# Phase tiles in a pool of their own, reused at the end for the last chunk's transform constants

## The chip, the cores and the metric

The kernel runs on one core of a Trainium2 chip. The metric is device time in microseconds (us), as the median of several executions; lower is better. One execution was also recorded by the hardware profiler, and that recording is what "the profile" and "the trace" mean below.

## What is computed

The reference is one transformer-like block on a sequence of 2048 rows of 640 features, in float32:

```python
mod = (_silu(c) @ w_mod).reshape(c.shape[0], 6, 1, -1)
sa, ca, ga, sb, cb, gb = (mod[:, 0], mod[:, 1], mod[:, 2], mod[:, 3], mod[:, 4], mod[:, 5])
h = _layernorm(x, axis=-1) * (1 + ca) + sa
x = x + ga * _A_ref(h, A_A_re, A_A_im, A_B_re, A_B_im, A_C_re, A_C_im, A_log_dt, A_Dskip)
h = _layernorm(x, axis=-1) * (1 + cb) + sb
x = x + gb * _B_ref(h, B_w1, B_w3, B_w2)
```

`_A_ref` builds for each of the 640 features a convolution kernel K of length 2048, a sum over 128 complex exponentials, and convolves the sequence with it by Fourier transforms. `_B_ref` is a gated feed-forward layer with 1728 hidden units (`silu(h w1) * (h w3)`, then `w2`).

## The kernel before

**Stages.** The time falls into a front (parameters, first normalization), the convolution, and the feed-forward part. The convolution writes its result `zs` to device memory; the feed-forward part starts with reading it back.

**The convolution's two streams.** One stream makes the kernel K, 16 features a step, in 40 steps (`NS`), after the front in rounds of 4 steps whose order of instructions is written out by hand (the string `ROUND`). For two steps at a time GpSimd makes integer phases (`phases`, tile `ph`, 32 x 67 values per partition), ScalarE turns them into sines in place and into cosines (`cs`), and VectorE multiplies them into the exponentials `A` (the words A1 and A2, `imag1` and `imag2`; A2 of the odd step is the last reader of a phase tile). TensorE sums these (`kg`, tile `pk`), and two more steps bring the kernel's transform into `uk`. There are 20 phase tiles in 3 buffers, in the pool `tp`, which the tables share.

The other stream is the transform itself, for 5 chunks of 128 features, 8 ticks a chunk, one tick a step, 10 steps behind (`LAG`): tick g of chunk c runs at step 10 + 8c + g. A tick is

- `stage2`: 16 matmuls of `uk` with the constant `s2` of that g, into `p2`;
- `k_copy` on ScalarE (tile `kc`), `products` and `sums` on VectorE (`T`, `p2`, `Y`);
- `inverse1`: 16 matmuls of `Y` with the constant `i1` of that g, into `pz`;
- `z_store`: ScalarE copies `pz` into `zt` (2 buffers), and a DMA stores it to `zs`.

Chunks 0 to 3 and tick 0 of chunk 4 run inside the rounds, beside the kernel's steps. Ticks 1 to 7 of chunk 4, the last chunk, run after the rounds, in a loop of their own, with nothing beside them but the first pieces of the feed-forward part (`x_part`).

**The constants.** `s2` and `i1` depend on g alone, 256 KB each. Each is loaded anew for every tick by `stage2_load` and `inverse1_load`, from SyncE's queue (`nc.sync`), into a pool of 2 buffers (`fp`). A load therefore has to wait until the tick two before it has used its constant. The dictionary `ahead` lets a load be made earlier: `stage2` and `inverse1` first look there.

**Names in the profile.** Digits are dropped from names there, so `s2` reads `s`, `i1` reads `i`, `p2` reads `p`. Most instructions carry line 109 (a helper); loads of `s2` carry L686, of `i1` L692, the loads `uk<-us` of the next chunk's input L678, the stores `zs<-zt` L766 (and, for the last chunk, ScalarE's queue).

**Orders.** Computing engines keep the program's order in this stretch. SyncE's DMAs are placed in its queue by the scheduler, and SyncE issues them strictly one after another: where one waits, those behind it wait too. After the last `i1` come, tied to it by `issue_after`, the first two weight tiles (`rw`) and two tiles of `x` (`xm`).

**Memory.** Pools are stacked from both ends: `tp` on the left, gone when the steps are done (`tabs.close()`); `kp`, then `fp`, on the right, gone when the convolution is done (`ssm.close()`). The feed-forward pools `xp` and `wq` are laid over them.

Of the kernel before, what the change touches and what calls it, by code (L numbers as in the profile page):

```python
# [9 lines left out]
F32 = mybir.dt.float32  # L10
F32R = mybir.dt.float32r
I32 = mybir.dt.int32
# [5 lines left out]
P = 128  # L18
# [5 lines left out]
NDC = D // DC  # L24
SD = 16
# [9 lines left out]
NPG = NPH + NG - 1  # L35
# [56 lines left out]
def bc(ap, axis, n):  # L92
    v = ap.unsqueeze(axis)
    shape = list(v.shape)
    shape[axis] = n
    return v.broadcast_to(shape)
# [18 lines left out]
def tile_kernel(ctx: ExitStack, tc: tile.TileContext, a):  # L115
    nc = tc.nc
# [22 lines left out]
    def keep(ins):  # L139

        return tc.keep_in_program_order(ins) if in_order[0] else ins
# [22 lines left out]
    ssm = ExitStack()  # L164
# [7 lines left out]
    one4 = kp.tile([P, 1], F32, name="one4")  # L172
    cT = kp.tile([P, KD], F32, name="cT")
    uk = kp.tile([P, 3, NA, DC], F32, name="uk")

    psS = ssm.enter_context(tc.tile_pool(name="psS", bufs=1, space=PSUM))

# [2 lines left out]
    tp = tabs.enter_context(tc.tile_pool(name="tp", bufs=2, reuse_waits="tile"))  # L180
# [251 lines left out]
    def late_load(i):  # L432

        late[i] = w_load(xw[:, :KD * WC].rearrange("p (k c) -> p k c", k=KD), 1920 + i * WC)
# [108 lines left out]
    ph, cs, AA, EC, PK, K1 = {}, {}, {}, {}, {}, {}  # L543
# [39 lines left out]

    def phases(s):
        sl = slice(s * SD, s * SD + 2 * SD)
        p = tp.tile([P, 2 * SD, NPG], I32, name="ph", bufs=3)
        hold = tc.keep_in_program_order if 0 < s < 4 else keep
        b0 = NA - 8
        base = p[:, :, b0:NA]
        hold(G.tensor_tensor(p[:, :, b0:], bc(thi[:, sl], 2, NPG - b0), bc(iota, 1, 2 * SD), op=OP.mult))  # L590
        keep(G.tensor_tensor(base, base, bc(phi[:, sl], 2, 8), op=OP.add))
        keep(G.tensor_tensor(p[:, :, :b0].rearrange("p k (g j) -> p k g j", j=8), bc(base, 2, NG - 1),
                             bc(p[:, :, NPH:], 3, 8), op=OP.add))
        ph[s] = p[:, :, :NPH]
# [86 lines left out]
    ahead = {}  # L681
# [7 lines left out]
    def inverse1_load(g):  # L689

        i1 = fp.tile([P, 2, 2, P], F32, name="i1")
        i1_last[0] = nc.sync.dma_start(i1, a["i1"][:, g * 2:g * 2 + 2])  # L692
        return i1

    def stage2(ch, g):
        s2 = ahead.pop((ch, g, "s2"), None)
        if s2 is None:
            s2 = stage2_load(g)
        kn = 1 + ch % 2

        n = ch * 8 + g
        p2 = psS.tile([P, 2, 2, 2 * DC], F32, name="p2", tag="B" if n > NS - 12 and n % 2 else "A", bufs=1)
        for pi in range(2):
            for c in range(2):
                for par in range(2):
                    f = g * 4 + pi * 2 + par
                    keep(PE.matmul(p2[par * 64:par * 64 + 64, pi, c, :], s2[:, pi * 2 + par, c * 64:c * 64 + 64],
                                   uk[:, 0:kn + 1:kn, f, :], start=True, stop=True, tile_position=(0, par * 64)))
        Pq[ch, g] = p2
        if g % 2 == 1 and ch + 1 < NDC:  # L710
            u_load(ch + 1, g // 2)
# [26 lines left out]
    def inverse1(ch, g):  # L738
        i1 = ahead.pop((ch, g, "i1"), None)
        if i1 is None:  # L740
            i1 = inverse1_load(g)
        Y = Yq.pop((ch, g))
        if g % 2 == 0:
            Zq[ch] = psS.tile([P, 2, 4, DC], F32, name="pz", tag="Z", bufs=1)
        pz = Zq[ch]
        for pi in range(2):
            for c in range(2):
                for par in range(2):
                    r = slice(par * 64, par * 64 + 64)
                    ins = keep(PE.matmul(pz[:, par, (g % 2) * 2 + pi, :], i1[r, pi, c, :], Y[r, pi, c, :],  # L750
                                         start=(c == 0), stop=(c == 1), tile_position=(par * 64, 0)))
        return ins
# [34 lines left out]
    def z_load(z, j, ks, q=nc.sync, b0=0):  # L787

        nb = z.shape[1]
        for k in ks:  # L790
            hh = int(k > 1)
            kk = k - 2 * hh
            q.dma_start(z[hh * 64:hh * 64 + 64, :, kk * DC:kk * DC + DC],
                        zsv[:, 4 * j + b0:4 * j + b0 + nb, k])
# [7 lines left out]
    def z_tile():  # L802
        z = tz.tile([P, SD, 3, NA], F32, name="A")
        return z.rearrange("p k s b -> p (k s b)").rearrange("p (b d) -> p b d", b=4)
# [15 lines left out]
    def x_load(j):  # L820
        xe.append(xw[:, j * D:(j + 1) * D])
        nc.sync.dma_start(xe[j], a["x"][j * P:(j + 1) * P, :])
# [21 lines left out]
    def conv_part(fn):  # L844
        return lambda k: fn((k - LAG) // 8, (k - LAG) % 8)

    parts = {"PH": phases, "AB": absph, "CO": cosine, "SI": sine, "PA": lambda k: exp_fast((k,)), "XA": fast,
             "PQ": lambda k: exp_slow((k,)), "XQ": slow, "E1": real1, "E2": real2, "A1": imag1, "A2": imag2,
             "kg": kgen, "K": k1evac, "pt": k_stage1, "uk": k_out}
# [5 lines left out]
    def do(name, k):  # L855

        lo, hi = (LAG, LAG + 8 * NDC) if name in conv else (0, NS)
        if name in by_two and k % 2:
            return None
        if front[0]:  # L860
            assert (name, k) not in done and lo <= k < hi, (name, k)
        if (name, k) in done or not lo <= k < hi or (name == "zt" and k % 2 == 0 and k < LAG + 8 * NDC - 8):
            return None
        done.add((name, k))
        return (conv if name in conv else parts)[name](k)
# [20 lines left out]
    def u_first(i):  # L886

        u_load(0, i)
        if i == 0:
            ahead[0, 1, "s2"] = stage2_load(1)  # L890
            for g in range(2):
                ahead[0, g, "i1"] = inverse1_load(g)
# [45 lines left out]
    for word in FRONT:  # L938
        name, k = word[:2].rstrip("+"), int(word[len(word[:2].rstrip("+")):])
# [25 lines left out]
    for rnd in range(NS // EB):  # L965
        if 2 <= rnd < 7:
            late_load(rnd - 2)
        for word in ROUND:
            name, k = word[:2].rstrip("+-"), EB * rnd + int(word[len(word[:2].rstrip("+-")):])
            if name in pieces:  # L970
                if 2 <= rnd < 7:
                    pieces[name](rnd - 2)
                continue
            do(name, k)
            if name == "E1" and 30 <= k < 38 and k % 2 == 0:
                x_load((k - 30) // 2)

            if name == "kg" and 36 <= k < 40:
                early.append((None, z_tile()))
                z_load(early[-1][1], k - 36, range(3), q=nc.gpsimd)  # L980
    in_order[0] = False

    for tk in range(NS + 1, LAG + 8 * NDC + 2):
# [13 lines left out]
        i = tk - 1 - LAG - 8 * NDC + 8  # L997
# [190 lines left out]
    ahead = {(0, n): w for n, w in first_w.items()}  # L1188
# [272 lines left out]
    for pair in range(2):  # L1461
# [4 lines left out]
        side = []  # L1466
# [8 lines left out]
        if pair == 0:  # L1475
            tiles = []
            power = x_first(tiles)
            for k in range(KD):
# [12 lines left out]
            side = [lambda: mid(0), lambda: (mid(1), mid(2)), lambda: mid(3), lambda: None,  # L1491
                    lambda: turn(4, 0, 2), lambda: turn(3, 1)]
# [106 lines left out]
```

## Time and profile before

| | us |
|---|---|
| runs: median (lowest to highest of 3) | 943.66 (943.36 to 947.34) |
| profiled execution, first to last instruction | 944.4 |
| TensorE, busy time | 876.6 |
| VectorE | 698.5 |
| ScalarE | 541.9 |
| GpSimd | 270.0 |

The profile gives no other time of the profiled execution than its span, and the span lies within the range of the runs. Three views are used. A timeline gives for each group of instructions on an engine its start, its duration, the engine, the line in the source, the operation, the tiles written and read, and in brackets the idle time before it with what ended it. The chain of waits follows the work that ended last back through what released it. The table by windows gives, for each stretch, its length, the busy time of each engine with the number of instructions, the clock granted to TensorE, the busy share of the DMA engines and their GB/s. PE is TensorE, DVE VectorE, ACT ScalarE, POOL GpSimd and SP SyncE; a "q" after the name means its queue, which issues DMAs.

### The profile page before, as it was taken

Reading aid. Unit: us, or ns where it says so; the run is one execution under the profiler, and the core shown is the slowest. Engines: PE = TensorE matmul, PEld = TensorE weight load, DVE = VectorE, ACT = ScalarE, POOL = GpSimd, SP = SyncE. Lnnn points to the kernel's source line nnn. Section 1 sums busy time; section 2 is a strip of 40 time slices with the busy share of each in tenths; the row PEclk is TensorE's granted clock in tenths of the full one; section 3 lists DMA queues with packets and bytes.
Section 4 is the critical chain, followed back from the end, with each engine's and each line's share of the span. In section 5 each row is a group of like instructions: output and inputs, shape, how many; then the busy total and the mean of one; then the engine's idle time right before and its main releaser. Section 6 shows DMA issues by size and latency. Waiting matters only on the chain.

```text
span 944.4 us, 19982 instructions
## 1 busy us (share of the span) xinstructions
PE 876.6 (93%) x7950; PEld 666.8 (71%) x7950; DVE 698.5 (74%) x1209; ACT 541.9 (57%) x747; POOL 270.0 (29%) x277
## 2 busy tenths in 40 slices
PE   3888889999988878999999999999999999999997
PEld 2545466666666655678888887578888888888886
DVE  5899889999999956676666655677876666664674
ACT  6988889999999532464333333465543333333332
POOL 3333434554453111223222201320342222200341
PEclk9967789999999999999999999999999999999999
DMA  9664396766666986863111126946311311123352
GB/s 273 210 223 175 129 212 180 206 191 168 213 199 181 223 245 201 236 227 98 56 45 53 46 71 207 279 151 182 126 57 57 111 56 57 57 82 99 98 194 84
DMA packets 104048, 140.68 MB, mean 149 GB/s; under 512 B 21044, under 2 KB 63156, under 8 KB 103956
## 3 DMA queue, kind: packets, MB, share of 16 engines
q1 hardware_dynamic: 93172, 113.59, 40.1%
q10 hardware_dynamic: 8480, 18.09, 6.1%
q0 software_dynamic: 2304, 7.74, 2.7%
q8 instruction: 62, 1.02, 0.4%
q14 instruction: 30, 0.25, 0.1%
HBM read 107.92 MB, written 31.46 MB: 148 GB/s over the span
## 4 chain that ended last, share of the span: by engine, by line
PE 72%; ACT 10%; DVE 7%; DMA 4%; SPq 4%; issue 3%; DVEq 0%; ACTq 0%
PE ps L109 52%; PE p L109 7%; SPq L109 3%; PE pz L109 3%; PE pt L109 3%; PE pk L109 2%; PE pa L109 2%; ACT cs L109 2%; PE pu L109 2%; ACT A L109 2%; DMA s<-in_s_dram 1%; DVE uk L109 1%; ACT ph L109 1%; ACT uk L109 1%; DVE u L109 1%
## 5 line engine op out<-in xcount | busy, mean ns | idle before, releaser
L109 DVE TENSOR_TENSOR s<-ps,s 128x512 f32<-128x512 f32 x138 | 94.9, 688 | 83.2 <-PE ps L109 82.9
L109 ACT CAST gh<-rw 128x640 fp32r<-128x640 f32 x87 | 63.4, 728 | 128.4 <-PE ps L109 86.1
L109 DVE TENSOR_TENSOR gl<-rw,gh 128x640 fp32r<-128x640 f32 x87 | 76.8, 883 | 70.5 <-ACT gh L109 70.5
L109 POOL TENSOR_TENSOR S<-rw 128x256 f32<-128x256 f32 x46 | 36.8, 802 | 234.4 <-DVE S0l L109 158.2
L109 PE MATMUL p<-uk,s 128*64 128x256 f32 x640 | 80.8, 396 | 19.9 <-DMA s<-in_s_dram 5.8
L109 PE MATMUL ps<-xA,gh 128*128 128x512 f32 x280 | 87.6, 391 | 0.4 <-ACT xA L109 0.4
L109 PE MATMUL ps<-gh,uh 128*128 128x512 f32 x224 | 87.6, 391 | 0.0
L109 PE MATMUL ps<-gl,uh 128*128 128x512 f32 x224 | 87.2, 389 | 0.0
L109 POOL TENSOR_TENSOR ph<-thi,iota 128x1376 int32<-128x1376 int32 x20 | 51.2, 2560 | 118.3 <-DVE A L109 103.6
L109 DVE TENSOR_TENSOR E<-A,cs 128x1024 f32<-128x1024 f32 (+1 forms) x80 | 80.6, 1018 | 2.2 <-PE pk L109 1.3
L109 PE MATMUL ps<-gh,ul 128*128 128x512 f32 x208 | 81.1, 390 | 0.0
L109 PEld LDWEIGHTS p<-uk,s 128*64 128x64 f32 x640 | 46.7, 140 | 44.2 <-issue 8.1
L109 ACT ACTIVATE A<-pa 128x1024 f32<-128x1024 f32 (+1 forms) x80 | 64.3, 815 | 9.9 <-PE pa L109 9.6
L109 PEld LDWEIGHTS ps<-xA,gh 128*128 128x128 f32 x280 | 52.3, 188 | 12.9 <-ACT xA L109 1.0
L109 DVE TENSOR_TENSOR A<-A,ph 128x1024 f32<-128x1024 f32 x40 | 54.1, 1357 | 0.8
L109 PE MATMUL ps<-xA,gl 128*128 128x512 f32 x140 | 54.5, 389 | 0.0
L109 PE MATMUL pt<-s,K 128*64 128x128 f32 x640 | 45.0, 284 | 6.1 <-ACT uk L109 5.9
L109 PEld LDWEIGHTS ps<-gh,uh 128*128 128x128 f32 x224 | 42.0, 188 | 9.3 <-DVE h L109 0.6
L109 PEld LDWEIGHTS ps<-gl,uh 128*128 128x128 f32 x224 | 42.1, 188 | 8.9
L109 PE MATMUL pz<-Y,i 64*128 64x128 f32 x640 | 46.5, 285 | 1.6 <-ACT zt L109 1.6
L109 PEld LDWEIGHTS pz<-Y,i 64*128 64x128 f32 x640 | 38.9, 187 | 12.0 <-issue 8.4
L109 POOL TENSOR_TENSOR rw<-rw,gbr 128x512 f32<-128x512 f32 x14 | 21.8, 1561 | 84.9 <-DMA rw<-in_w_dram 83.0
(214 smaller groups left out, 2179.3 us busy)
## 6 DMA issues: line engine op xcount, KB each, us to landing
rw<-in_w_dram ACTq DMA_DIRECT2D x44, 320.0 KB
us<-u SPq DMA_DIRECT2D x16, 640.0 KB
s<-in_s_dram SPq DMA_DIRECT2D x40, 256.0 KB
i<-in_i_dram SPq DMA_DIRECT2D x40, 256.0 KB
rw<-in_wg_dram SPq DMA_DIRECT2D x31, 320.0 KB
rw<-in_wu_dram SPq DMA_DIRECT2D x28, 320.0 KB
uk<-us SPq DMA_DIRECT2D x32, 256.0 KB
zs<-zt SPq DMA_DIRECT2D x32, 256.0 KB
```

The source lines that it names most:

```text
L109: ins = fn(*args, **kw)
```

## The change

The phase tiles get a pool `php` of their own, 3 buffers as before, on the right side above `kp`, so that it lives as long as the convolution. When the 20 phase tiles are used up, three more tiles are taken from it, after A2 of steps 35, 37 and 39. Each holds `s2` and `i1` of two ticks of the last chunk, four loads of 256 KB, and they are entered in `ahead`. So ticks 0 to 5 of the last chunk find their constants there, and ticks 6 and 7 alone load theirs into `fp`.

```diff
+    php = ssm.enter_context(tc.tile_pool(name="php", bufs=3, side="right", reuse_waits="tile"))
+
+    def phase_tile():
+        return php.tile([P, 2 * SD, NPG], I32, name="ph")
...
     def phases(s):
         sl = slice(s * SD, s * SD + 2 * SD)
-        p = tp.tile([P, 2 * SD, NPG], I32, name="ph", bufs=3)
+        p = phase_tile()
...
+    def last_pairs(g0):
+
+        t = phase_tile().rearrange("p k b -> p (k b)").bitcast(F32)
+        for i in range(4):
+            g, half = g0 + i // 2, t[:, i * 4 * P:i * 4 * P + 4 * P]
+            name, src, n = (("s2", a["s2"], 4), ("i1", a["i1"], 2))[i % 2]
+            v = half.rearrange("p (f c) -> p f c", f=4) if n == 4 else half.rearrange("p (f h c) -> p f h c", f=2, h=2)
+            nc.sync.dma_start(v, src[:, g * n:g * n + n])
+            ahead[NDC - 1, g, name] = v
...
             do(name, k)
+            if name == "A2" and k in (35, 37, 39):
+                last_pairs(k - 35)
```

On TensorE, VectorE, ScalarE and GpSimd the order of the instructions stays as it was; on TensorE the matmuls of ticks 0 to 5 read `ph` where they read `s2` and `i1`. SyncE's queue changes. Here is what stands in it around step 37 before; the first `s` is that of tick 5 of chunk 3:

```order
L766 DMA zs<-zt 64x1024 x2
L678 DMA uk<-us 64x8x128 x2
L686 DMA s_4202<-in_s_dram 128x512
L692 DMA i_4296<-in_i_dram 128x512
L686 DMA s_4344<-in_s_dram 128x512
L692 DMA i_4358<-in_i_dram 128x512
```

and the same place in the changed kernel, where the four `ph` are the second batch of constants:

```order
L780 DMA zs<-zt 64x1024 x2
L682 DMA uk<-us 64x8x128 x2
L706 DMA ph<-in_s_dram 128x512
L706 DMA ph<-in_i_dram 128x512
L706 DMA ph<-in_s_dram 128x512
L706 DMA ph<-in_i_dram 128x512
L690 DMA s_4215<-in_s_dram 128x512
L696 DMA i_4314<-in_i_dram 128x512
L690 DMA s_4362<-in_s_dram 128x512
L696 DMA i_4376<-in_i_dram 128x512
```

The batch stands between the loads `uk` and the `s` of tick 5, and nothing else has moved there; the first and the third batch stand ahead of the `s` of ticks 3 and 7 in the same way. The other place is the end of the last chunk. Before, from the `i` of its tick 3 and the `s` of its tick 5 on, the constants alternate down to the `i` of tick 7, and the weights `rw` and tiles `xm` follow:

```order
L692 DMA i_4586<-in_i_dram 128x512
L686 DMA s_4607<-in_s_dram 128x512
L692 DMA i_4620<-in_i_dram 128x512
L686 DMA s_4658<-in_s_dram 128x512
L692 DMA i_4671<-in_i_dram 128x512
L686 DMA s_4716<-in_s_dram 128x512
L692 DMA i_4729<-in_i_dram 128x512
L692 DMA i_4750<-in_i_dram 128x512
L810 DMA rw<-in_wg_dram 128x640
L810 DMA rw<-in_wu_dram 128x640
L1011 DMA xm<-in_x_dram 128x640 x2
L775 DMA zs<-zt 64x512
```

In the changed kernel, from the `s` of chunk 3's tick 7 on (the first row; the second `s` and the third belong to ticks 6 and 7 of the last chunk):

```order
L690 DMA s_4398<-in_s_dram 128x512
L696 DMA i_4426<-in_i_dram 128x512
L690 DMA s_4654<-in_s_dram 128x512
L696 DMA i_4449<-in_i_dram 128x512
L780 DMA zs<-zt 64x1024 x2
L682 DMA uk<-us 64x8x128 x2
L690 DMA s_4710<-in_s_dram 128x512
L696 DMA i_4723<-in_i_dram 128x512
L696 DMA i_4744<-in_i_dram 128x512
L780 DMA zs<-zt 64x1024 x2
L824 DMA rw<-in_wg_dram 128x640
L824 DMA rw<-in_wu_dram 128x640
```

Only the constants of the last two ticks are left, the stores of chunk 3's last pair of ticks now stand behind the last `i`, and the weights and the tiles of `x` follow at once.

In memory, `tp` shrinks by the three phase tiles and `fp` moves down by as much. The feed-forward tiles keep their places, so they lie over other tiles than before: the split weights `gh`, `gl`, `uh`, `ul` over `xw`, `s2`, `i1` and `kc`, where they lay over the tables.

## The prediction

> **What bounds the kernel now.** I read the page first, then the chain of waits around the end of the convolution, then the timelines of TensorE and of SyncE's queue there, then a table by windows.
>
> ```profile
> span 944.4 us, 19982 instructions
> PE 876.6 (93%) x7950; PEld 666.8 (71%) x7950; DVE 698.5 (74%) x1209; ACT 541.9 (57%) x747; POOL 270.0 (29%) x277
> ```
>
> TensorE is busy for 93% of the span. So a change that does not shorten matmuls can win only where TensorE waits, and the change touches one such place: the last chunk's second stage (`p<-uk,s`, 16 matmuls a tick), which multiplies by the constant `s`. Its ticks in TensorE's timeline (start, duration, wait before it), from tick 3 of chunk 3 on:
>
> ```profile
> 309.81 1.95 PE L109 MATMUL p<-uk,s 128*64 128x256 f32 x16 [0.94 <-DVE Y L109]
> ...
> 321.48 1.95 PE L109 MATMUL p<-uk,s 128*64 128x256 f32 x16
> 329.32 1.95 PE L109 MATMUL p<-uk,s 128*64 128x256 f32 x16
> 332.29 1.95 PE L109 MATMUL p<-uk,s 128*64 128x256 f32 x16
> 336.13 1.95 PE L109 MATMUL p<-uk,s 128*64 128x256 f32 x16
> 340.89 1.95 PE L109 MATMUL p<-uk,s 128*64 128x256 f32 x16 [1.72 <-DMA s<-in_s_dram]
> 343.86 1.95 PE L109 MATMUL p<-uk,s 128*64 128x256 f32 x16
> 347.85 1.95 PE L109 MATMUL p<-uk,s 128*64 128x256 f32 x16 [0.95 <-DMA s<-in_s_dram]
> 354.02 3.30 PE L109 MATMUL p<-uk,s 128*64 128x256 f32 x16 [3.13 <-DMA s<-in_s_dram]
> 358.34 1.95 PE L109 MATMUL p<-uk,s 128*64 128x256 f32 x16
> ```
>
> 336.13 is tick 0 of the last chunk, 332.29 is tick 7 of chunk 3. Ticks 1, 3 and 4 of the last chunk wait for the load of `s`. The chain of waits (start, duration, what) passes through two of these loads and then through the end of the convolution:
>
> ```profile
> 336.44 4.32 DMA s<-in_s_dram
> ...
> 345.85 8.13 DMA s<-in_s_dram
> ...
> 354.02 3.30 PE p L109 x16
> ...
> 371.94 5.42 DMA zs<-zt
> ...
> 377.41 1.99 DMA A<-zs
> 379.40 0.14 issue
> 379.53 8.13 PE ps L109 x57
> ```
>
> Each `s` has two buffers and is loaded when the tick two before it has released one. While a tick takes 5 to 10 us, that is early enough. Here a tick lasts 343.86 - 340.89 = 2.97 us when nothing is late, and a load of 4.32 to 8.13 us is not covered. What follows 371.94 is one chain (store, reload, matmuls), so whatever the ticks gain reaches the end of the kernel.
>
> **The change part by part.** *Removed: the waits.* 1.72 + 0.95 + 3.13 = 5.80 us. The tick after the longest wait also took 3.30 us instead of 1.95. In the table by windows (busy time of each engine, then granted clock, share of the DMA engines, GB/s) the clock is low there:
>
> ```profile
> 354.00:356.00 2.00, 1.98 (x10) 1.22 (x12) 0.00 (x0) 0.00 (x0) 0.00 (x0) 0.50 0.67 167
> ```
>
> The 1.35 us go with the wait, so the part removed is worth 5.80 + 1.35 = 7.15 us, if nothing else is late. Next in line is the chain inside a tick (ACT's copy `kc`, DVE's products and sums); ticks 1 to 2 already ran at 2.97 us with all of it.
>
> *Added and moved: the loads.* The last chunk's sixteen loads of 256 KB stay sixteen; none is added. Twelve of them leave the last chunk's stretch and go earlier in three batches of four (1.05 MB each), and each batch stands in SyncE's queue ahead of an `s` that chunk 3 still needs. The batch waits until DVE has read the phase tile for the last time (the scalar_tensor_tensor of odd steps 35, 37, 39):
>
> ```profile
> 301.61 0.68 DVE L109 SCALAR_TENSOR_TENSOR A<-ph,A 128x512 f32<-128x512 f32 x1
> ...
> 312.74 0.69 DVE L109 SCALAR_TENSOR_TENSOR A<-ph,A 128x512 f32<-128x512 f32 x1
> ...
> 326.38 0.68 DVE L109 SCALAR_TENSOR_TENSOR A<-ph,A 128x512 f32<-128x512 f32 x1
> ```
>
> So the batches can go at 302.3, 313.4 and 327.1. The `s` behind each was issued, in SyncE's timeline, at
>
> ```profile
> 301.10 0.59 SPq L686 DMA_DIRECT2D s<-in_s_dram  x1
> ...
> 313.19 0.61 SPq L686 DMA_DIRECT2D s<-in_s_dram  x1
> ...
> 325.63 0.70 SPq L686 DMA_DIRECT2D s<-in_s_dram  x1
> ...
> 342.87 0.33 SPq L686 DMA_DIRECT2D s<-in_s_dram  x1
> ```
>
> (the first three rows; the last shows what an issue costs SyncE when its queue is free) and needed at 309.81, 321.48 and 332.29, ticks 3, 5 and 7 of chunk 3, none of which waited for it. Queued behind each batch are also an `i`, a pair of stores `zs` and a pair of loads `uk`; these are used a tick or more later than the `s`. How full the DMA engines are in those stretches:
>
> ```profile
> 301.00:306.00 5.00, 4.91 (x108) 3.60 (x106) 4.90 (x9) 3.99 (x5) 0.00 (x0) 1.00 0.96 277
> 306.00:308.00 2.00, 1.97 (x22) 1.20 (x20) 1.68 (x3) 1.88 (x4) 1.85 (x4) 1.00 0.24 84
> 308.00:322.00 14.00, 11.46 (x240) 8.65 (x240) 13.04 (x23) 9.94 (x11) 3.03 (x5) 1.00 1.01 248
> ...
> 330.00:334.00 4.00, 4.00 (x44) 2.75 (x42) 2.04 (x5) 1.60 (x2) 0.00 (x0) 1.00 0.43 136
> ...
> 370.00:372.00 2.00, 1.82 (x32) 1.24 (x32) 0.32 (x2) 0.58 (x1) 1.53 (x3) 1.00 1.02 396
> ```
>
> A batch of 1.05 MB takes 2.65 us at the highest of these rates (396 GB/s) and 4.2 us at 248. TensorE takes its work in order, so a late `s` stops everything behind it, and DVE, busy 13.04 of 14 us in the middle stretch, cannot make it up: a late `s` costs its lateness.
>
> First batch: the engines fall to 0.24 in 306 to 308, so what was issued before had landed by about 306.5 (2 us x 0.24). Behind 1.05 MB this `s` lands at 309.2 to 310.3 (306.5 plus 2.65, or plus 3.8 at 277 GB/s), against 309.81. Cost 0 to 0.5; I take 0.3.
>
> Second batch: the engines are full (1.01), so the queue decides. The one transfer whose landing the profile tells at this moment is GpSimd's, in the list of DMA issues (count, KB, us to landing) for 313 to 314:
>
> ```profile
> A<-zs POOLq DMA_DIRECT2D x2, 128.0 KB, 7.2
> ```
>
> With 7.2 us the `s` landed at 320.4. In the changed kernel it starts 0.24 us later (313.43 for 313.19) and behind 2.65 to 4.2 us of constants: 323.3 to 324.8, against 321.48, a cost of 1.8 to 3.4. With 4.32 us instead (the chain's shorter load) it would land at 320.4 to 322.0, a cost of 0 to 0.5; with 8.13 at 324.2 to 325.8, a cost of up to 4.3, and from a wait of 3.13 on the low clock's 1.35 may come again. I take 2.6, from the row of that moment.
>
> Third batch: it can go 327.06 - 325.63 = 1.4 us later than the `s` it now precedes. Four issues at 0.33 to 0.61 us add 1.3 to 2.4, so the `s` goes at 328.4 to 329.5. At 4.32 us it lands at 332.7 to 333.8, a cost of 0.4 to 1.5. If the engines first work off what they had (at 0.43 over 330 to 334, so until about 331.7) and then the batch, it lands at 334.4 to 335.9, a cost of 2.1 to 3.6. I take 1.2, nearer the first, since the second batch's delay also gives the queue time.
>
> *The end of the chunk.* The two loads of weights and the two of `x` now stand behind the last `i` at about 341 instead of 365 us (SyncE's timeline):
>
> ```profile
> 361.42 3.89 SPq L692 DMA_DIRECT2D i<-in_i_dram  x2
> 365.41 0.37 SPq L810 DMA_DIRECT2D rw<-in_wg_dram  x1
> ```
>
> They replace constants in a stretch that moves 273 GB/s, so the stores of `zs` there meet about the same traffic. Those stores matter, because ACT's copy `zt` waits for the store of two ticks before:
>
> ```profile
> 344.59 1.47 ACTq L109 DMA_DIRECT2D zs<-zt  x2
> ...
> 353.00 0.58 ACT L109 COPY zt<-pz 128x512 f32<-128x512 f32 x1 [2.59 <-DMA zs<-zt]
> ...
> 359.07 1.10 ACTq L109 DMA_DIRECT2D zs<-zt  x2
> 361.42 0.58 ACT L109 COPY zt<-pz 128x512 f32<-128x512 f32 x1 [0.51 <-PE pz L109]
> ...
> 364.99 0.58 ACT L109 COPY zt<-pz 128x512 f32<-128x512 f32 x1 [0.51 <-PE pz L109]
> ```
>
> The first of them took 353.00 - 344.59 = 8.4 us, one in the quieter stretch at most 364.99 - 359.07 = 5.9. A copy comes due 5.94 us (two ticks) after the one of two ticks before, and that one's store is issued 0.61 us after it began. With 8.4 us the copy is 8.4 + 0.61 - 5.94 = 3.1 us late; `kc` of the next tick stands behind it, its 0.58 and the store's issue of 1.10, and was due 1.95 us after the copy, so it is 2.8 us late; with 5.9 us, 0.3. I put 0 here, with 0 to 2.8 as the bounds, since the stores that follow the stretch are fast. The phase tiles' new place in memory adds no instruction; the weights' split tiles now lie over `xw`, `s` and `i`, which are dead before ACT reaches them. I put 0.
>
> Sum against the profiled execution (944.4 us first to last instruction; the runs' median of 943.66 lies 0.7 below, so I subtract from the median): -7.15 + 0.3 + 2.6 + 1.2 + 0 = -3.05 us, that is 940.6 us.
>
> [...]
>
> **The rivals.** (1) The batches are absorbed: loads land so early in chunk 3 that 1 MB more is hidden. For it: none of the three `s` waited. Against: 1.01 of the DMA engines in use. It gives the full 7.15, 936.5 us. (2) Slower: SyncE's queue holds the `s` of ticks 5 and 7 back by the whole transfer of the batch and by the later issue too. The second then costs 4.2 of transfer and 2.6 of issue (313.43 + 2.4 - 313.19), less a slack of 1.1 (8.29 from issue to use, 7.2 to landing), 5.7; the third 4.2 and 3.8 with no slack (6.66 to use), 8.0. Together 13.7: 943.66 - 7.15 + 13.7 = 950.2. It decides from 7.15 us for the two, 3.6 each, and is slower by over 0.5% from 11.9. For it: the row of 1.01. Against it: the engines work off a batch while its last loads are still being issued, so transfer and issue do not add up. (3) The stores of `zs` become the bound in the ticks that now run at 2.97 us: 2.8 us at one or two places, on top of my sum, 943.4 to 946.2. For it: the copy's wait of 2.59. Against: at 361.42 and 364.99 it waits for `pz` alone. (4) It does nothing, because the constants would wait too: excluded by the release at 302 to 327, before 336.
>
> **How the numbers follow.** My forecast (part of the gain handed back in chunk 3) 0.60; absorbed 0.20; stores 0.12; slower 0.08. About 0.5%, 4.7 us, is what a measurement of this kernel can tell from no change. Faster by more: rival 1 and the fifth of my forecast where the batches cost under 2.4 in all, 0.20 + 0.12 = 0.32. Slower by more: 0.08. The rest, 0.60, is within. The range takes in rival 1 with 1 us of less traffic at the last store, and the upper bounds of the batches (0.5 + 4.3 + 3.6 = 8.4, 944.9) with part of rival 3: 935.5 to 946.5.
>
> **What would show it.** Right: no wait for `s` before the last chunk's ticks 1 to 5, spaced by about 2.97 us; a new wait of 1.8 to 3.4 us before tick 5 of chunk 3 and of 0.4 to 3.6 before tick 7; almost none before tick 3; the clock at 1.00 through the chunk. It is wrong if chunk 3 shows no wait for `s` (rival 1), waits of over 4 us at two of the three places (rival 2), or `zt` waiting for `zs` by over 3 us (rival 3).

## The result, and the profile after

The changed kernel takes 952.23 us (median of 6 runs, 949.17 to 957.89) against 943.51 us for the kernel before (6 runs beside it, 942.58 to 947.34). The ratio is 1.0076 with a 95% interval of 1.0051 to 1.0101: slower by 7.2 us, where 940.6 and a small gain were forecast. Measured a second time, on another chip, the ratio is 1.0077 (1.0050 to 1.0103).

The head of the page says that TensorE has no more to do than before (873.9 us busy for 876.6); the time is in its waits:

```profile
span 949.0 us, 19961 instructions
...
PE 873.9 (92%) x7950; PEld 662.7 (70%) x7950; DVE 699.9 (74%) x1209; ACT 541.1 (57%) x747; POOL 267.9 (28%) x277
```

TensorE's timeline of the changed kernel, the matmuls `p` of the ticks as in the prediction (start, duration, wait before it and what ended it), from tick 3 of chunk 3 on; the rows `p<-uk,ph` are ticks 0 to 5 of the last chunk:

```profile
307.97 1.95 PE L109 MATMUL p<-uk,s 128*64 128x256 f32 x16 [1.18 <-DMA s<-in_s_dram]
...
324.39 3.42 PE L109 MATMUL p<-uk,s 128*64 128x256 f32 x16 [4.90 <-DMA s<-in_s_dram]
...
333.70 1.95 PE L109 MATMUL p<-uk,s 128*64 128x256 f32 x16
339.17 1.95 PE L109 MATMUL p<-uk,s 128*64 128x256 f32 x16 [2.43 <-DMA s<-in_s_dram]
343.01 1.95 PE L109 MATMUL p<-uk,ph 128*64 128x256 f32 x16
345.98 1.95 PE L109 MATMUL p<-uk,ph 128*64 128x256 f32 x16
...
358.14 1.95 PE L109 MATMUL p<-uk,ph 128*64 128x256 f32 x16
...
371.47 1.94 PE L109 MATMUL pz<-Y,i 64*128 64x128 f32 x16 [2.29 <-issue]
...
377.42 4.61 PE L109 MATMUL ps<-idle 128*128 128x512 f32 x10 [0.98 <-DVE xm L109]
```

Set each start against that of the same tick before. Tick 3 of chunk 3 starts 1.84 us earlier (307.97 for 309.81), tick 5 2.91 later, tick 6 4.38 later, tick 7 and tick 0 of the last chunk 6.88 later: chunk 3 has lost 8.72 us. Tick 5 of the last chunk starts 0.20 earlier (358.14 for 358.34): the ticks without waits have given 7.08 us back. More loss comes behind that. The last `pz` waits 2.29 us (1.55 before) and runs at the low clock, as do the idle matmuls (`ps<-idle`, whose result nothing uses), which take 4.61 us (2.55 before).

The chain of waits shows how the `s` of ticks 5 and 7 came to be late:

```profile
307.45 7.66 DMA zs<-zt
315.12 9.22 DMA s<-in_s_dram
324.39 3.42 PE p L109 x16
...
334.17 4.96 DMA s<-in_s_dram
339.17 1.95 PE p L109 x16
...
353.14 6.73 DMA zs<-zt
359.94 0.59 ACT zt L109
```

and SyncE's timeline there, with the second batch:

```profile
311.40 0.52 SPq L706 DMA_DIRECT2D ph<-in_s_dram  x1
311.97 0.42 SPq L706 DMA_DIRECT2D ph<-in_i_dram  x1
312.45 0.42 SPq L706 DMA_DIRECT2D ph<-in_s_dram  x1
313.86 0.33 SPq L706 DMA_DIRECT2D ph<-in_i_dram  x1
315.12 0.50 SPq L690 DMA_DIRECT2D s<-in_s_dram  x1
```

The `s` of tick 5 is issued at 315.12, 3.72 us after the batch began. The four issues of the batch take 1.69 us of that; most of the rest is SyncE waiting for earlier DMAs to land (1.0 us for an `i`, 0.9 for a store of `zs`). The last of these waits is in the chain: the `s` goes out as a store of `zs` of 307.45 lands (307.45 + 7.66 = 315.11). The table by windows (length, busy time of PE, PEld, DVE, ACT, POOL, then granted clock, DMA share, GB/s) shows full DMA engines around TensorE's wait, the clock at half behind it, and a second stretch at half clock at the end:

```profile
314.00:324.00 10.00, 5.09 (x112) 4.03 (x112) 8.24 (x13) 2.09 (x3) 0.00 (x0) 1.00 1.08 277
324.00:326.00 2.00, 1.61 (x8) 1.00 (x10) 0.00 (x0) 0.00 (x0) 0.00 (x0) 0.50 0.90 330
...
372.00:382.00 10.00, 8.45 (x58) 4.95 (x61) 4.63 (x14) 1.94 (x3) 1.77 (x4) 0.50 0.30 84
```

At the end of the chunk, SyncE issues the first weights and tiles of `x` at 348.37 to 350.95 (365.41 in the kernel before), and ScalarE's copies `zt` then wait for stores of `zs`:

```profile
348.37 0.80 SPq L824 DMA_DIRECT2D rw<-in_wg_dram  x1
349.21 0.74 SPq L824 DMA_DIRECT2D rw<-in_wu_dram  x1
350.00 0.95 SPq L1027 DMA_DIRECT2D xm<-in_x_dram  x2
```

```profile
356.41 0.59 ACT L109 COPY zt<-pz 128x512 f32<-128x512 f32 x1 [1.91 <-DMA zs<-zt]
...
359.94 0.59 ACT L109 COPY zt<-pz 128x512 f32<-128x512 f32 x1 [1.13 <-DMA zs<-zt]
```

### The profile page after: what moved, and what is told of

The parts are those of the page before. It is cut to its first block, busy times and chain, and to the rows that moved or that the text cites. A ratio compares the mean times of both kernels' runs of the same rounds, so it can differ in the third digit from the quotient of the medians.

```text
span 949.0 us, 19961 instructions
## 1 busy us (share of the span) xinstructions
PE 873.9 (92%) x7950; PEld 662.7 (70%) x7950; DVE 699.9 (74%) x1209; ACT 541.1 (57%) x747; POOL 267.9 (28%) x277
## 4 chain that ended last, share of the span: by engine, by line
PE 66%; ACT 10%; DVE 9%; DMA 6%; issue 4%; SPq 3%; POOL 1%; ACTq 0%; DVEq 0%; POOLq 0%
PE ps L109 49%; PE p L109 6%; PE pz L109 3%; PE pt L109 3%; SPq L109 3%; PE pk L109 2%; PE pa L109 2%; ACT cs L109 2%; DMA zs<-zt 2%; ACT A L109 1%; DMA s<-in_s_dram 1%; DVE uk L109 1%; ACT uk L109 1%; DVE A L109 1%; ACT ph L109 1%
## 5 line engine op out<-in xcount | busy, mean ns | idle before, releaser
L109 PE MATMUL p<-uk,s 128*64 128x256 f32 x544 | 69.6, 397 | 22.0 <-DMA s<-in_s_dram 8.5
L109 PEld LDWEIGHTS p<-uk,s 128*64 128x64 f32 x544 | 39.7, 141 | 43.8 <-issue 7.8
L109 PEld LDWEIGHTS pt<-s,K 128*64 128x64 f32 x640 | 36.1, 142 | 14.4 <-ACT uk L109 8.5
L109 ACT ACTIVATE s<-ps 128x512 f32<-128x512 f32 (+1 forms) x33 | 19.7, 596 | 44.7 <-PE ps L109 42.9
L109 PEld LDWEIGHTS ps<-gh,ul 128*128 128x128 f32 x208 | 39.0, 188 | 8.4
```

The costliest lines, as they stand in the source:

```text
L109: ins = fn(*args, **kw)
```

## The experiments

**How they are read.** The runs of one kernel lie some 8 us apart (31 runs of the kernel before on one chip: 940.76 to 948.91), so a trace, which is one execution, is not compared by its span. Two stretches of it are compared instead: *chunk 3*, from the start of its tick 2 to the start of tick 0 of the last chunk, and *the last chunk*, from there to the first matmul `ps<-A`, which reads the stored `zs` back. In the kernel before these rows are

```profile
304.88 1.95 PE L109 MATMUL p<-uk,s 128*64 128x256 f32 x16
...
374.41 2.55 PE L109 MATMUL ps<-idle 128*128 128x512 f32 x10 [0.98 <-DVE xm L109]
379.53 1.62 PE L109 MATMUL ps<-A,i 64*32 64x128 f32 x32 [2.57 <-DMA A<-zs]
```

so chunk 3 is 336.13 - 304.88 = 31.25 and the last chunk 379.53 - 336.13 = 43.40. Over three traces without early loads (the kernel before twice, and the one with the new pool alone) chunk 3 is 31.25, 31.27 and 31.27, the last chunk 43.40, 40.66 and 41.77; their sum is 73.2 on average. Without early loads, then, chunk 3 repeats within 0.02 us, the last chunk only within 2.7. For every kernel, in us; the last two columns are the ratio to the kernel before with its interval, and that in us of 944:

| kernel | chunk 3 | last chunk | sum less 73.2 | ratio (95%) | us |
|---|---|---|---|---|---|
| changed, first trace | 40.22 | 38.95 | +6.0 | 1.0076 (1.0051 to 1.0101) | +7.2 |
| changed, second trace | 41.33 | 37.09 | +5.2 | 1.0077 (1.0050 to 1.0103) | +7.3 |
| pool alone | 31.27 | 41.77 | -0.2 | 1.0005 (0.9986 to 1.0025) | +0.5 |
| loads unused | 42.43 | 42.73 | +12.0 | 1.0102 (1.0077 to 1.0126) | +9.6 |
| first batch | 33.35 | 38.09 | -1.8 | 0.9989 (0.9970 to 1.0008) | -1.0 |
| one batch for all | 32.20 | 37.15 | -3.9 | 0.9981 (0.9962 to 1.0000) | -1.8 |
| first and second | 37.58 | 34.96 | -0.7 | 1.0010 (0.9989 to 1.0030) | +0.9 |
| first and a later one | 33.58 | 36.72 | -2.9 | 0.9978 (0.9959 to 0.9998) | -2.1 |
| GpSimd's queue | 38.82 | 36.37 | +2.0 | 1.0054 (1.0033 to 1.0074) | +5.1 |
| batches behind `s` | 35.91 | 36.87 | -0.4 | 0.9952 (0.9932 to 0.9972) | -4.5 |
| weights held back | 42.52 | 35.80 | +5.1 | 1.0040 (1.0021 to 1.0060) | +3.8 |
| both | 32.71 | 35.41 | -5.1 | 0.9965 (0.9945 to 0.9984) | -3.3 |
| later one, weights held | 35.87 | 34.92 | -2.4 | 0.9975 (0.9955 to 0.9995) | -2.4 |
| two far back, first kept | 33.63 | 38.89 | -0.7 | 0.9993 (0.9975 to 1.0011) | -0.7 |
| two batches at step 41 | 31.26 | 41.13 | -0.8 | 1.0009 (0.9988 to 1.0029) | +0.8 |
| the same, parts later | 31.26 | 41.99 | 0.0 | 1.0001 (0.9982 to 1.0020) | +0.1 |

The sums follow the times within 2.5 us but for two rows (GpSimd's queue 3.1, batches behind `s` 4.1). So these two stretches account for the times to within 2 to 4 us, and finer differences between rows are not read from them.

**The kernel before, a second trace.** No edit.

> The kernel before, profiled a second time, to see how far two executions of one program differ. Expected: the same waits for s in the last chunk to within 0.5 us, the first 131 us up to 2 us earlier or later, and the span within 3 us of 944.4. If the matmuls behind the convolution (386 to 414 us) run without gaps again, the 2 to 3 us that all changed kernels lose there are an effect of the changes; if they show gaps, they are scatter.

Measured: span 944.6. TensorE's timeline of its last chunk:

```profile
339.96 3.14 PE L109 MATMUL p<-uk,s 128*64 128x256 f32 x16 [2.22 <-DMA s<-in_s_dram]
...
347.81 1.95 PE L109 MATMUL p<-uk,s 128*64 128x256 f32 x16 [0.23 <-DMA s<-in_s_dram]
352.07 1.95 PE L109 MATMUL p<-uk,s 128*64 128x256 f32 x16 [0.35 <-DMA s<-in_s_dram]
355.04 1.95 PE L109 MATMUL p<-uk,s 128*64 128x256 f32 x16
```

The waits differ by more than the 0.5 us expected: 2.80 us in all where the first trace had 5.80. From tick 0 to tick 5 it is 20.34 us, in the first trace 22.21, in that of the pool alone 22.06; without any wait it is 14.85 (5 ticks of 2.97). So waits and low clock there are worth 5.5, 7.4 and 7.2. The matmuls behind the convolution showed a gap in this trace (1.55 us at 411) where the first had none, so such gaps come without the change too.

**The changed kernel, a second trace.** No edit.

> The changed kernel a second time, on one chip with the two kernels above. Expected: the ratio to the kernel before again 1.005 to 1.010; the wait before tick 5 of chunk 3 again 4 to 6 us, before tick 7 2 to 3. If the ratio comes out under 1.003, the first result was partly the chip's scatter.

Measured: ratio 1.0077, as expected. TensorE waits 3.12 us before tick 3, 3.20 before tick 5, which is under the 4 to 6 expected, and 2.97 before tick 7. The `s` of tick 5 is again issued late: 7.49 us after the start of tick 3 (318.31 for 310.82), where it was 3.38 in the kernel before (313.19 for 309.81).

**The pool alone.**

```diff
-            if name == "A2" and k in (35, 37, 39):
-                last_pairs(k - 35)
```

> Only the pool of the phase tiles and with it their place in memory is changed; no constant is loaded early. Theory (queue order: the second and third batch hold up the s of chunk 3's ticks 5 and 7, about 9 us with the low clock behind the first of these waits): 943.5, within 1 us of the kernel before, with the waits for s in the last chunk still there. Rival A (the new place in memory costs by itself): up to 952 without any early load.

Measured: 946.01 us, ratio 1.0005. The phase tiles' new place in memory costs nothing that can be measured; rival A falls.

**The loads without their use.** The ticks of the last chunk load their own constants as before.

```diff
             nc.sync.dma_start(v, src[:, g * n:g * n + n])
-            ahead[NDC - 1, g, name] = v
```

> The three batches are loaded as in the change, but the last chunk's ticks do not use them and load their own constants as before, so the early loads are pure cost (twelve loads of 256 KB more than before). Theory (batches ahead of chunk 3's s): waits of 4 to 6 us before tick 5 and 2 to 3 before tick 7 of chunk 3, and about 9 us slower than before, 950 to 954. Rival (the changed kernel's loss is made at the end of the convolution, where it has no loads of its own left and ticks run at 2.97 us): within 3 us of before.

Measured: 954.54 us, ratio 1.0102, just above the 950 to 954 expected. The early loads alone cost 9.6 us, in chunk 3 (42.43 for 31.26); the last chunk is as before. The scheduler put the batches otherwise than in the change (the third goes at 316.46, where it went at 331.34), and the long wait is not before ticks 5 and 7, as expected, but one tick earlier, for an `i` that stands behind the second batch:

```profile
324.60 2.08 PE L109 MATMUL pz<-Y,i 64*128 64x128 f32 x16 [6.75 <-DMA i<-in_i_dram]
```

So loads in front of chunk 3's own cost that much without any change in the last chunk, and that the whole loss is made at the end of the convolution is excluded.

**The gain without the second and third batch.** Ticks 2 to 5 use the constants of ticks 0 and 1 again, so the kernel leaves out eight loads and the right values of these ticks.

```diff
+                for g in range(2, 6):
+                    for n in ("s2", "i1"):
+                        ahead[NDC - 1, g, n] = ahead[NDC - 1, g % 2, n]
```

> Only the first batch is loaded, and ticks 2 to 5 of the last chunk use the constants of ticks 0 and 1 over again, so eight loads (2 MB) and the right values of those ticks are left out. Theory: the end of the convolution has its whole gain without the second and third batch's cost, about 7 us, 936.5; if the late stores of zs and the low clock after the convolution (some 2 to 3 us in the changed kernel) are brought by the shorter last chunk itself, 939. Rival C (the loss is made at the end of the convolution and after it): 943 or more.

Measured: 942.99 us, ratio 0.9981. Its last chunk is 37.15 us, 4.8 less than the 41.94 of the three traces, and the first batch takes 0.9 in chunk 3. So the shorter last chunk keeps 4.8 of the 6.7 that its waits are worth on average, and in time the whole is -1.8 (-3.6 to 0). Both values expected (936.5 and 939) were too low, and the time lies at the edge of the rival's 943; the loads without their use, above, are what speaks against that rival.

**Which batch.** The first alone (`k == 35`); the first and second (`k in (35, 37)`); the first and the third (`k in (35, 39)`).

> The pool and only the first batch (constants of ticks 0 and 1 at step 35). Theory: no wait over 1.5 us before ticks 3, 5 and 7 of chunk 3, the wait before tick 1 of the last chunk (1.72) gone, those before ticks 3 and 4 partly left: 939 to 942. Rival B (any early batch disturbs chunk 3, by the DMA engines' load and not by its place in the queue): 943 to 948.

> The first and the second batch as in the change, without the third (ticks 4 and 5 of the last chunk load their constants as before). Theory: the second batch is the dear one, a wait of 3 to 5 us before tick 5 of chunk 3 and up to 1.5 on the low clock; without the third the wait before tick 7 is under 0.5: 947 to 950. Rival (first and second batch are absorbed alone, only three in a row are too much): 943 or less.

> The first and the third batch as in the change, without the second (ticks 2 and 3 of the last chunk load their constants as before). Theory: waits as with one batch before ticks 3 and 5, and 2 to 3 before tick 7: 944 to 947. Rival (the third batch costs nothing where the second has not made chunk 3 late): 941 to 943.5.

Measured: 943.33 (0.9989), 945.66 (1.0010) and 942.41 us (0.9978). The first missed its 939 to 942. It costs 2.1 us of chunk 3 in its trace (33.35) where 0.3 was forecast, more than the 0.25 of the changed kernel's first trace and as much as in its second; the profile puts the wait there (2.89 us before tick 3) down to VectorE and not to the `s`. With the second, tick 5 of chunk 3 waits as in the change, and the weights are issued late again:

```profile
326.06 3.57 PE L109 MATMUL p<-uk,s 128*64 128x256 f32 x16 [4.64 <-DMA s<-in_s_dram]
```

```profile
364.25 0.37 SPq L824 DMA_DIRECT2D rw<-in_wg_dram  x1
```

It is the dear batch (37.58 - 33.35 = 4.2 us more in chunk 3), as the theory had it; but two batches came out below the 947 to 950 expected, since the last chunk gave more back (34.96) than in the change (38.95). The kernel meant for the third batch turned out another experiment: taken second, the batch got the second tile, and the scheduler placed it right *behind* the `s` of tick 5, at 314.25 for 313.52. There it cost 0.2 us more than the first batch alone (33.58 for 33.35) and no low clock (tick 5 took 1.95 us), though that tick still waited 2.26 us for its `s`. That made the place in the queue, and not the bytes, the suspect.

**One place back.** All three batches; the second and third are issued one place later, behind the `s` of ticks 5 and 7 and not ahead of it. The first, at 36 for 35 in the edit, keeps its place in the queue.

```diff
-            if name == "A2" and k in (35, 37, 39):
-                last_pairs(k - 35)
+            if name == "A2" and k in (36, 39, 41):
+                last_pairs(2 * (36, 39, 41).index(k))
```

> All three batches; the second and the third are each issued one place later on SyncE, right behind the s of ticks 5 and 7 of chunk 3 instead of right ahead of it. Theory (place in the queue): the waits before ticks 5 and 7, 3 to 5 and 2 to 3 us in the changed kernel, fall to under 2.5 and under 1, the low clock behind tick 5 goes, and the time falls by 4 to 6 us against the changed kernel, 945 to 948. Rival (the bytes fill the DMA engines whatever the place): waits and time as in the changed kernel, 950 to 953.

Measured: 941.93 us (7 runs, 941.37 to 943.21), ratio 0.9952 (0.9932 to 0.9972): 4.5 us faster than the kernel before, and 1.0077 - 0.9952 = 0.0125, 11.8 us, faster than the change (about 8.5 to 15 by the two intervals). SyncE's queue at the second batch, and TensorE's tick 5, of this kernel:

```profile
312.38 0.61 SPq L690 DMA_DIRECT2D s<-in_s_dram  x1
313.10 0.36 SPq L706 DMA_DIRECT2D ph<-in_s_dram  x1
```

```profile
308.52 2.48 PE L109 MATMUL p<-uk,s 128*64 128x256 f32 x16 [2.27 <-DVE A L109]
...
320.11 1.95 PE L109 MATMUL p<-uk,s 128*64 128x256 f32 x16
```

The same bytes go through the same queue at nearly the same time (the batch begins 4.6 us after the start of tick 3, in the change 3.4), and tick 5 does not wait. This shows the cause in chunk 3: the place in the queue. The time fell by more than expected, and by more than this one trace accounts for. Its two stretches are only 6.4 and 5.6 us shorter than in the two traces of the change: ahead of tick 6 TensorE stands still for 1.23 us, for which no view names a cause, and runs at the low clock behind that (0.71 from 326 to 328, 0.50 from 328 to 330). The kernel "both" of the table, with the same queue in chunk 3, has no such gap (32.71 for 35.91), but waits 1.34 us before tick 5.

**Another queue.**

```diff
-            nc.sync.dma_start(v, src[:, g * n:g * n + n])
+            nc.gpsimd.dma_start(v, src[:, g * n:g * n + n])
```

> All three batches as in the change, but issued from GpSimd's queue and not SyncE's. Theory in its narrow form (SyncE's four issues and its queue order hold s up): the waits before ticks 5 and 7 of chunk 3 shrink to under 2 us together, 940 to 945. Rival B (the DMA engines are full, whichever queue carries the batch): the waits stay at 4 to 7 us together, 950 to 954.

Measured: 949.88 us, ratio 1.0054. SyncE issues the `s` of tick 5 on time and ahead of GpSimd's batch (the second row is its first load), and it still comes late:

```profile
309.71 0.61 SPq L690 DMA_DIRECT2D s<-in_s_dram  x1
```

```profile
310.51 0.56 POOL L706 DMA_DIRECT2D ph<-in_s_dram  x1
```

```profile
323.23 3.68 PE L109 MATMUL p<-uk,s 128*64 128x256 f32 x16 [5.10 <-DMA s<-in_s_dram]
```

From issue to use are 13.5 us, against 7.7 in the kernel above (320.11 - 312.38). The wait before tick 7 is gone: there the `s` goes out at 328.30, before the third batch (331.70), and not behind it (334.17 in the change). So each theory has one place: at tick 7 it was SyncE's order, and at tick 5 a batch in another queue delays the `s`, though the `s` is issued first. Behind the `s` in its own queue the batch leaves it at 7.7 us from issue to use, and tick 5 without a wait; beside it in another queue it is 13.5 us, and a wait of 5.10. That the batch's bytes are what delays the `s` there is the author's reading; how the engines divide their time between the two queues was not shown.

Within SyncE's queue, what the place changes is the issue and hardly the landing. In the change the `s` of tick 5 lands 9.22 us after its issue. In "first and a later one", where the batch stands behind the `s`, and in "two far back" (below), where no second batch is near, the chains of waits have

```profile
313.52 9.44 DMA s<-in_s_dram
```

```profile
312.40 8.96 DMA s<-in_s_dram
```

But in both the `s` goes out 3.33 us after the start of tick 3, in the kernel one place back 3.86, in the change 7.15 (315.12 - 307.97). Landing as slowly, it makes tick 5 wait 2.26 and 1.92 us in these two, for 4.90 in the change.

**The weights held back.** In the changed kernel, the four loads of weights and `x` are issued by GpSimd once VectorE has made `Y` of tick 5.

```diff
+            mark.append(G.tensor_copy(mk, Yq[NDC - 1, 5][:, 0, 0, 0:1]))
...
-        with tc.issue_after(i1_last[0].ins):
-            w_get(first_w[name], 0, name)
+        with tc.issue_after(mark[0].ins):
+            w_get(first_w[name], 0, name, q=nc.gpsimd)
```

> The changed kernel, with the first two loads of weights and two of x held back from about 348 to about 360 us (issued by GpSimd once DVE has made the products of tick 5). Theory (these 1.3 MB delay the stores of zs, and by them the copies zt, the products and the clock): no wait of zt for a store in the last chunk, stores land within 3.5 us, and 2 to 3 us are won against the changed kernel, 949 to 950.5. Rival (the ticks themselves are too fast for the stores): the waits of zt stay, 951 to 953.

Measured: 950.15 us, ratio 1.0040; against the change's 1.0076 that is 3.4 us, give or take 3. They were issued at 364.53, later than meant, and `zt` no longer waits for a store:

```profile
356.89 0.59 ACT L109 COPY zt<-pz 128x512 f32<-128x512 f32 x1 [0.51 <-PE pz L109]
...
359.86 0.59 ACT L109 COPY zt<-pz 128x512 f32<-128x512 f32 x1 [0.51 <-PE pz L109]
```

The last chunk is 35.80 us, for 38.95 and 37.09 in the two traces of the change. The same edit on two other kernels:

> Both edits, the second and third batch behind their s and the weights held back. Theory: the two gains add up, 942 to 945, at or below the kernel before. Rival (what is won in front is given back behind the convolution): 946 to 949.

> The first batch and the one of ticks 4 and 5 behind the s of tick 5 (ticks 2 and 3 load theirs as before), with the weights held back. Without the holding back it was 0.998 of before. Theory: 1 to 2 us less than that, 939.5 to 941.5. Rival: the same time, 942 to 943.5.

Measured: 942.83 us (0.9965) and 943.75 (0.9975), against 0.9952 and 0.9978 without the holding back. In the traces the last chunk gets shorter here too (36.87 to 35.41, 36.72 to 34.92), in the times there is no difference outside the intervals. The first expectation held (942 to 945), the second failed (939.5 to 941.5). So early weights cost some 1.3 to 3.2 us at the end of the convolution, and what becomes of them in the time is not settled. No version is measurably faster than the one with the batches one place back.

**Far back.** Second and third batch at step 41, behind every `s` of chunk 3, with the first batch kept; then only two batches there, for ticks 1 to 4; then the same with DVE's first two parts of the next stage one tick later. The edit is that of the last kernel; the first has 2 and 4 in place of the 1 and 3, and the first two leave `x_part` as it was.

```diff
+            if name == "st" and k == 41:
+                for g0, ins in ((1, s2_last[0]), (3, uk_last[0])):
+                    with tc.issue_after(ins.ins):
+                        last_pairs(g0)
...
-            for j in ((), (), (), (), (0,), (1,), (), (2, 3))[i]:
+            for j in ((), (), (), (), (), (0,), (1,), (2, 3))[i]:
```

> The first batch as in the change; the second and third are issued at step 41 behind the last s and uk that chunk 3 loads, so that nothing of chunk 3 stands behind them. Theory: no wait for s before ticks 5 and 7 of chunk 3, and the time of the kernel with one batch reused, 941 to 944. Rival (batches of 1 MB hurt wherever they stand, by the stores of zs and the clock): 946 or more.

> Two batches only, for ticks 1 and 2 and for ticks 3 and 4, both issued at step 41 behind every s of chunk 3; tick 0 and tick 5 load theirs as before. Theory: chunk 3 as in the kernel before, with no new wait, and the last chunk without waits for s; 5 to 7 us earlier at its end, of which the stretch behind it gives 3 to 5 back (as with one batch reused): 940 to 942.5. Rival (the whole gain reaches the end once chunk 3 is free): 937 to 939.

> As the kernel with two batches at step 41, and DVE takes the first two parts of the next stage (sums on the reloaded zs) one tick later each, behind the products of ticks 6 and 7 and not ahead of them. Theory (the fixed order on DVE makes tick 7 wait for the reload, TensorE then idles and its clock falls): the wait of 2.3 before the last pz shrinks to under 1, and 1 to 2 us are won against the kernel with two batches: 939 to 941. Rival (the stretch behind is set by its own transfers): no difference over 0.5 us in time.

Measured: 944.40 (0.9993), 945.93 (1.0009) and 945.69 us (1.0001). The first, just above the 941 to 944 expected, has its gain eaten by waits for `s` before ticks 3 and 5 of chunk 3 (2.64 and 1.92 us) behind the first batch, which the theory had not expected at tick 5, and by the early weights. In the second chunk 3 is free, exactly as before (31.26), yet the last chunk gains 0.8 only, and the expectation of 940 to 942.5 failed: the second batch now stands, at 333.37 to 335.4 us, ahead of the last chunk's own `i` and of a pair of stores, and there are waits instead.

```profile
343.10 1.16 PE L109 MATMUL pz<-Y,i 64*128 64x128 f32 x16 [0.66 <-DMA i<-in_i_dram]
344.93 1.16 PE L109 MATMUL pz<-Y,ph 64*128 64x128 f32 x16 [0.68 <-ACT zt L109]
...
348.83 2.08 PE L109 MATMUL pz<-Y,ph 64*128 64x128 f32 x16 [2.74 <-DVE Y L109]
```

It is again the place in the queue, but by the chain of waits not the batch's: the `i` goes out at 338.21, behind the stores of 336.68, which wait for ScalarE's copy `zt`; the later two waits follow from that one, through ScalarE and VectorE. The third kernel missed its 939 to 941, and tells nothing on its own question, since the same waits come before the place that it changes.

## Why the prediction was wrong, step by step

**The part removed** was right. 7.15 us were forecast; between tick 0 and tick 5 of the last chunk the change took 7.08 out, and ticks 0 to 4 are spaced by 2.97, as forecast. That it comes so near is in part luck: over three traces without early loads the waits there are worth 5.5 to 7.4. And "whatever the ticks gain reaches the end" did not hold: in the kernel with one batch for all, 4.8 of 6.7 did.

**First batch**: 0.3 forecast, with 0.5 as its bound. In the change's first trace tick 2 to tick 3 grew by 0.25 us (5.18 for 4.93), in its second by 2.2, with the first batch alone in chunk 3 by 2.1. The bound was too low. The wait before tick 3 was between 1.18 and 3.12 us in two executions of one program (0.94 before); what makes it so different was not tried.

**Second batch**: this is the step that failed, forecast at 2.6 and measured at 6.2. The prediction put "it starts 0.24 us later (313.43 for 313.19)", counted the four issues for the third batch, and left them at nothing for the second. Tick 3 started 1.84 us earlier, so in step with it the `s` was due to go out at 311.35; it went out at 315.12, 3.77 later. From issue to use it took 9.27 us, where it was 8.29 before: 0.98 more. Together this is the 4.75 by which tick 5 came later in step with tick 3. The low clock, named as something that "may come again" and put at nothing in the 2.6, took 1.47 more: 6.2 in all. The transfer, which the forecast did count, was the smaller part: "7.2 us" and "2.65 to 4.2 us of constants" make 9.85 to 11.4 for the landing, 9.22 was measured, and a kernel without the second batch there has 8.96. Adding the issue to the forecast's 2.6 would give about 6.1; that this is near the 6.2 is chance, since the 6.2 holds 1.47 of low clock.

**Third batch**: 1.2 forecast, 2.43 measured as a wait, within the bounds of 0.4 to 3.6. Here the issue was counted.

**End of the chunk**: "I put 0 here, with 0 to 2.8 as the bounds". The prediction saw that the weights would come at about 341 (348 in the trace), but took them for as much traffic as the constants that they replace, and trusted the stores behind. The `zt` waits of 1.91 and 1.13 and the longer way to the end (38.95 and 37.09 us, with the weights held back 35.80) make it 1.3 to 3.2.

**The sum**: forecast -7.15 + 4.1 = -3.05. By the two stretches it is +9.0 in chunk 3 and -3.0 in the last chunk in the first trace, +10.1 and -4.9 in the second, +5.6 on average; measured +7.2.

**The rivals.** Rival 2 named the later issue, and its second batch (5.7) is nearer to the 4.75 than the forecast's 2.6. It was held at 0.08 because "transfer and issue do not add up". They did not add up in full, but the issue alone counts against the `s` behind the batch, which cannot be transferred before it is issued. Its third batch (8.0) was too dear, as that `s` landed after 4.96 us, and it had nothing for the end of the chunk; so it is luck that its 950.2 lies near the measured 952.2. Its sign, waits of over 4 us at two places, came at one (4.90). Part of rival 3 came as well, on top of it, where the prediction gave the two as alternatives: `zt` waited 1.91 and 1.13 us for a store, under the 3 us named as its sign. Absorption (rival 1) is excluded by the wait of 4.90 and by the loads without their use, +9.6 us.

**What stays open.** Why the kernel with the batches one place back is 4 us faster in its runs than its one trace says: the profiled execution itself took 942.63 us, so that part of the gain lies outside the two stretches, or is scatter. ("Both", with the same queue in chunk 3, is 2 us slower than its stretches say.) And where SyncE's wait inside the second batch comes from: the `s` went out at 315.12, as a store landed (315.11) that stood eight DMAs ahead of it in SyncE's queue; why it waited for that store was not shown, and no kernel here varied it.

## What to carry to other kernels

An early load is not free because its data are not due yet: what counted here was who stood behind it in the queue, and when that one was due. Place it behind the next load that something waits for; here one place made the difference between 1.0077 and 0.9952, of which about half shows in the stretches of the traces. Count a batch's issues, and the waits of the issuing engine among them, against the load behind it (here that `s` was issued 3.77 us later in step, of the 4.75 by which tick 5 came later), and not its transfer alone; and where loads vanish at the end of a stage, look which ones move up into the gap, and which stores they meet (here `zt` waited 1.91 and 1.13 us for stores of `zs`).

## What the runs showed of the hardware that was not expected

Behind a short wait TensorE ran at a low clock in one execution and not in another; what decides it was not found. In the second trace of the kernel before a wait of 2.22 us was followed by a tick of 3.14 us instead of 1.95 (granted clock 0.51 from 342 to 344); in the second trace of the change one of 3.20 was followed by a tick of 1.95:

```profile
325.72 1.95 PE L109 MATMUL p<-uk,s 128*64 128x256 f32 x16 [3.20 <-DMA s<-in_s_dram]
```

Two executions of one program differed in a part by more than in the whole: the waits for `s` in the last chunk of the kernel before were 5.80 us in one and 2.80 in another, with spans of 944.4 and 944.6.
